# First two groups with float32r operands in both layers, and all weights turned into float16 in place during the second group

## The chip, the cores and the metric

The kernel runs on one core of one Trainium2 chip. The metric is the device time of one execution in microseconds. Engines are named as in the profile: PE multiplies matrices, PEld loads its stationary operand, DVE, ACT and POOL work on vectors, SP issues the transfers.

## The reference

`q`, `k` and `v` are float32 of shape 8 x 8 x 576 x 64 (batch, heads, positions, head size); `w_in` is 512 x 2048 and `w_out` 2048 x 512. `setup_inputs` draws `q` and `k` as normal numbers times 0.43 (0.1 x 4.30), `v` times 0.1, and the weights times one over the root of their first size.

```python
def _attn_ref(q, k, v):                      # attention inside chunks of 64 positions
    scores = scale * np.matmul(q_c, k_c.transpose(0, 1, 2, 4, 3))
    scores = scores - np.max(scores, axis=-1, keepdims=True)
    attn = np.exp(scores)
    attn = attn / (np.sum(attn, axis=-1, keepdims=True) + 1e-09)
    out = np.matmul(attn, v_c)
...
def _moe_ref(x, w_in, w_out):
    h = x @ w_in
    g = h - np.tanh(h)
    return (g @ w_out).astype(np.float32)
...
    x = np.ascontiguousarray(attn_out.transpose(0, 2, 1, 3)).reshape(B * S, H * D)
    return _moe_ref(x=x, **moe_kwargs)
```

The attention output of all heads is a token matrix `x` of 4608 x 512, and two layers with `h - tanh(h)` between them follow.

## The kernel before

The 4608 tokens are nine groups of four tiles of 128 tokens. One tile is one "pair" of chunks: its attention gives 128 rows of `x`. A group goes through 16 units `fc`, each a block of 128 hidden features. Unit `fc` of a group is 12 matmuls of the first layer (`gemm1`, L466), the step between the layers on ACT and DVE (`shrink`, L477), and 12 matmuls of the second layer (`gemm2`, L494), two units behind the first (`LAG = 2`).

Each operand of a matmul is split into a high part `h` and a low part `l`, and a product is the three matmuls h·h, h·l and l·h. There are two kinds of split. In the float16 kind, the operand is first scaled by a power of two, which takes the size of the operand (`spread` L95 or `largest` L114 along the row, then a reduction over partitions on POOL, then three small DVE instructions in `power`, L101). In the float32r kind no power is needed: `h` is a copy into float32r, `l` is the difference.

- First layer, all groups: weights `wi` and tokens `x` are float16. The weights have one power for each pair of units (`to_w`, `from_w`), the tokens of the first two groups one for each group.
- Second layer, groups 0 and 1: weights `wo` and the inner values `gh`, `gl` are float32r. From group 2 on they are float16. The conversion of `wo` runs during group 1 (`Half`, L385 on): POOL adds the two parts (`convert`, L425), ACT makes the high part, DVE the low part.

The weights come as 64-bit numbers. `weights` (L139) puts the bits together in one ACT and three DVE instructions (`merged`, L132), then splits. For the first layer this takes two units at a time, because of their common power: `spread` on ACT (L153), POOL, DVE, and then L160 and L161. For the second layer L144 and L145 make the split.

Group 0 starts while weights and tokens still arrive. The attention of the first eight pairs (groups 0 and 1) is `Early`: it works in float32 on operands laid out by the host. The last step, `result` (L268), scales by the power of the group's `v`, found by `powers` (L203) with a `spread` of each of the four `v` tiles. From pair 8 on `Late` does the attention in float16, and its steps are put between the units of the group before (`interleaved`).

The order of group 0 is the string `PLAN`. Its tokens: `a` and `v` load a pair's operands, `l` loads weights, `c` puts them together, `S`, `M` or `E`, `N` or `n`, `T` and `V` are the steps of a pair's attention, `p` the power of a group, `g` is `gemm1` with `shrink`, `h` is `gemm2`, and `F` is a number of matmuls on zeros. Up to the `|` the order of SP and PE is as written. All else is ordered by the scheduler of the language, engine by engine, and on every engine instructions then run in that order. In units 0 to 3 of group 0 the tokens come in two halves of 256 (`g0.0` and `g0.1`), later all 512 together.

When the last weights are through, the memory of the raw weights (`raw_pool`) becomes the working memory of `Late` and `Half`. `Late` then has POOL set eight tiles of zeros (L287).

Of the kernel before, what the change touches and what calls it, by code (L numbers as in the profile page):

```python
# [13 lines left out]
BF16 = mybir.dt.bfloat16  # L14
F16 = mybir.dt.float16
# [6 lines left out]
P = 128  # L22
# [15 lines left out]
RAW = 3  # L38
EARLY_FC = 8
# [11 lines left out]
a0 a1 l0.0 l1.0 v0 v1 a2 v2 v3 p0 F4 F1 l0.1 F4 S0 S1 l1.1 F1 a3 F6 l2.0 l3.0 E0 c0.0 c1.0 N0 T0 S2 F4 M1 M2 n1 c0.1 T1 N2 V0 V1 F7 S3 T2 l2.1 g0.0 c1.1 M3 V2 l3.1 N3 T3 V3 | g1.0 c2.0 c3.0 a4 l4.0 l5.0 v4 g0.1 h c2.1 Y S4 l4.1 l5.1 g1.1 a6 g2.0 E4 c3.1 h n4 a5 c4.0 c5.0 h l6.0 l7.0 c4.1 g3.0 h v6 g2.1 h l6.1 l7.1 c5.1 S5 E5 g3.1 h g4 S6 E6 h N5 c6.0 c7.0 n6 g5 l8.0 l9.0 v5 a7 v7 p1 T4 h T5 c6.1 V5 c7.1 g6 T6 V4 h S7 E7 V6 N7 l8.1 l9.1 T7 V7 Z c8.0 c9.0 l10.0 l11.0 g7 h c8.1 g8 c9.1 h g9 l10.1 l11.1 c10.0 c11.0 h c10.1 l12.0 l13.0 c11.1 l12.1 c12.0 c13.0 g10 l13.1 h c12.1 g11 l14.0 l15.0 h g12 c13.1 l14.1 l15.1 c14.0 c15.0 h g13 c14.1 c15.1 h g14 h g15 h h h  # L51
# [3 lines left out]
def attn_ffn_kernel(ctx: ExitStack, tc: tile.TileContext, qE, kE, vE, qL, kL, vL, w_in, w_out, out):  # L55

# [32 lines left out]
    to_w = const.tile([P, FC // 2], F32, name="to_w")  # L89
    from_w = const.tile([P, FC // 2], F32, name="from_w")  # L90

    def new_x():
        return tuple(xpool.tile([P, KC, MOST], F16, name=f"x{a}") for a in "hl")

    def spread(pool, a, out):  # L95

        shape = [a.shape[0], *a.shape[1:]]
        junk = pool.tile(shape, BF16, name=f"junk{math.prod(shape[1:])}", bufs=1)
        nc.scalar.activation(junk, a, AF.Abs, scale=2.0 ** -12, accum_out=out)  # L99
# [20 lines left out]
    raw_in, raw_out, w_in_f, from_x, to_x = {}, {}, {}, {}, {}  # L120

    def load_weights(pool, fc, half):
        if half:
            raw_out[fc] = pool.tile([P, DM, 2], U32, name="raw_out", bufs=RAW)
            nc.sync.dma_start(out=raw_out[fc], in_=w_out[fc])
            return
        j, i = divmod(fc, 2)
        if i == 0:
            raw_in[j] = pool.tile([P, 2, DM, 2], U32, name="raw_in", bufs=2)
        nc.sync.dma_start(out=raw_in[j][:, i], in_=w_in[fc])  # L130

    def merged(w, raw):  # L132
        low, up = raw[:, :, 0], raw[:, :, 1]
# [4 lines left out]

    def weights(pool, fc, part):  # L139
        if part:  # L140
            w = pool.tile([P, DM], U32, name="w_out", bufs=2)
            merged(w, raw_out.pop(fc))
            w = w.bitcast(F32)
            nc.scalar.copy(out=wo[fc][0], in_=w)  # L144
            nc.vector.tensor_sub(wo[fc][1], w, wo[fc][0])  # L145
            return
        j, i = divmod(fc, 2)
        if i == 0:
            w_in_f[j] = pool.tile([P, 2, DM], U32, name="w_in", bufs=2), pool.tile([P, 2], F32, name="wsum", bufs=2)
# [21 lines left out]
    class Early:  # L171
# [104 lines left out]
    class Late:  # L276
# [4 lines left out]
        def __init__(self, pool):  # L281
# [4 lines left out]
            for t in self.v16[0] + self.v16[1] + self.q16[0] + self.q16[1]:  # L286
                nc.gpsimd.memset(t, 0.0)  # L287
# [5 lines left out]
        def sums(self, g, n):  # L293
# [5 lines left out]
            if n != "v":  # L299
                spread(self.pool, some, d["sums"][:, "qkv".index(n):"qkv".index(n) + 1])  # L300
                return
# [369 lines left out]
```

## Time and profile before

| what | us |
|---|---|
| median of 3 runs | 880.99 |
| lowest, highest | 880.87, 882.39 |
| profiled execution | 883.09 |
| its span, first to last instruction | 881.3 |
| PE busy in the span | 852.8 |
| DVE busy in the span | 595.5 |
| ACT busy in the span | 490.5 |
| POOL busy in the span | 39.9 |
| mean granted TensorE clock | 0.984 |

The profiled execution lies 2.1 us above the median. Busy time counts from an instruction's start to its end; matmuls overlap in the array, so a matmul's own duration is longer than the distance between two starts, and the distance is what a stream of them costs. A clock of 1.0 stands for 2.4 GHz.

### The profile page before, as it was taken

To read this page: it belongs to the slowest core of one execution; us is meant where nothing else is said; L and a number is where in the kernel's file an instruction comes from. 1 tells how busy PE (TensorE), PEld (TensorE's weight loads), DVE (VectorE), ACT (ScalarE), POOL (GpSimd) and SP (SyncE) were. 2 spreads that over 40 slices of the span, in tenths; PEclk is the share of its full clock that TensorE was granted. 3 is DMA by queue.
4 is the path that set the end of the run, shared out by engine and by line. 5 is a ranking of instruction groups with operands and counts; after the bars stand their busy time and mean duration, and the time that the engine had idled before them with its cause. 6 is when DMAs were issued, how large, how long until landed. Compare 5 with 4: busy or idle time off the path is not lost.

```text
span 881.3 us, 13271 instructions
## 1 busy us (share of the span) xinstructions
PE 852.8 (97%) x5162; PEld 459.1 (52%) x5163; DVE 595.5 (68%) x1056; ACT 490.5 (56%) x858; POOL 39.9 (5%) x49
## 2 busy tenths in 40 slices
PE   8899897999989999999999999999999999999997
PEld 5776754566664454445444544454445444544443
DVE  5698899898796685667666866586668666543222
ACT  7589674876574664465446544654465444333222
POOL 0000003122220000000000000000000000000000
PEclk9699998999999999999999999999999999999999
DMA  9657334122132212121212121212121011001001
GB/s 233 215 158 207 120 118 146 48 72 69 40 96 65 56 50 81 52 59 49 74 59 60 49 68 64 61 49 62 71 61 26 16 45 25 13 13 48 1 1 48
DMA packets 61375, 62.73 MB, mean 71 GB/s; under 512 B 32640, under 2 KB 40832, under 8 KB 61312
## 3 DMA queue, kind: packets, MB, share of 16 engines
q1 hardware_dynamic: 61312, 61.88, 24.0%
q8 instruction: 40, 0.66, 0.3%
q14 instruction: 23, 0.19, 0.1%
HBM read 45.09 MB, written 9.44 MB: 62 GB/s over the span
## 4 chain that ended last, share of the span: by engine, by line
PE 88%; ACT 5%; DVE 3%; DMA 3%; issue 1%; SPq 1%; POOL 0%; ACTq 0%; DVEq 0%; POOLq 0%
PE ph L473 40%; PE po L499 39%; PE psa L368 2%; PE psa L334 2%; ACT junk L99 2%; PE psa L266 2%; PE psa L218 1%; DMA raw_in<-w_in 1%; DVE w_out L135 1%; DMA rawv<-vL 1%; ACT s L236 1%; DMA rawk<-kL 1%; ACT wih L160 0%; DMA vbd<-vE 0%; ACT t L481 0%
## 5 line engine op out<-in xcount | busy, mean ns | idle before, releaser
L499 PE MATMUL po<-woh,gh 128*128 128x512 f16 (+1 forms) x1024 | 321.4, 385 | 3.3 <-ACT gh L490 3.3
L499 PE MATMUL po<-woh,gl 128*128 128x512 f16 (+1 forms) x576 | 219.8, 385 | 2.4 <-DVE gl L491 2.4
L473 PEld LDWEIGHTS <-wih 128*128 128x128 f16 x1184 | 113.1, 99 | 141.7 <-ACT wih L160 10.4
L481 ACT ACTIVATE t<-ph,sig 128x512 f32<-128x512 f32 (+1 forms) x148 | 99.5, 673 | 154.1 <-PE ph L473 151.4
L482 DVE SCALAR_TENSOR_TENSOR t<-ph,sig,t 128x512 f32<-128x512 f32 (+1 forms) x148 | 108.2, 732 | 112.1 <-ACT t L481 111.9
L473 PE MATMUL ph<-xh,wih 128*128 128x512 f16 (+1 forms) x592 | 150.5, 376 | 10.2 <-ACT wih L160 8.1
L473 PE MATMUL ph<-xh,wil 128*128 128x512 f16 (+1 forms) x592 | 150.5, 377 | 0.2 <-DVE wil L161 0.2
L473 PE MATMUL ph<-xl,wih 128*128 128x512 f16 (+1 forms) x592 | 149.4, 375 | 0.0
L486 DVE SCALAR_TENSOR_TENSOR gl<-t,to_g,gh 128x512 f16<-128x512 f32 x112 | 84.0, 750 | 90.5 <-ACT gh L485 89.6
L499 PEld LDWEIGHTS <-gh 128*128 128x128 f16 x896 | 85.6, 98 | 98.7
L485 ACT ACTIVATE gh<-t,to_g 128x512 f16<-128x512 f32 x112 | 80.6, 719 | 89.4 <-PE po L499 75.2
L473 PEld LDWEIGHTS <-wil 128*128 128x128 f16 x592 | 58.1, 99 | 67.7 <-issue 2.1
L499 PEld LDWEIGHTS <-gl 128*128 128x128 f16 x448 | 43.8, 98 | 52.9
L499 PE MATMUL po<-wol,gh 128*128 128x512 f32 x128 | 51.1, 399 | 0.0
L316 ACT ACTIVATE q16h<-rawq,to 64x512 f16<-64x512 f32 x56 | 40.2, 719 | 11.9 <-DVE to L112 9.8
L317 DVE SCALAR_TENSOR_TENSOR q16l<-rawq,to,q16h 64x512 f16<-64x512 f32 x56 | 43.7, 780 | 1.4
L326 DVE SCALAR_TENSOR_TENSOR v16l<-rawv,to,v16h 64x512 f16<-64x512 f32 x56 | 41.9, 749 | 1.1 <-ACT xh L371 0.2
L325 ACT ACTIVATE v16h<-rawv,to 64x512 f16<-64x512 f32 x56 | 40.0, 714 | 1.5 <-PE psa L368 0.8
L354 ACT CAST a<-s 128x512 f16<-128x512 f32 x28 | 17.3, 617 | 34.2 <-DVE s L348 34.0
L342 ACT ACTIVATE s<-s,exp 128x512 f32<-128x512 f32 x28 | 19.9, 712 | 20.8 <-DVE s L341 20.8
L499 PEld LDWEIGHTS po<-woh,gh 128*128 128x128 f32 x128 | 24.5, 191 | 11.5 <-ACT gh L490 5.5
L499 PEld LDWEIGHTS po<-woh,gl 128*128 128x128 f32 x128 | 24.3, 190 | 8.6 <-DVE gl L491 3.1
(122 smaller groups left out, 938.8 us busy)
## 6 DMA issues: line engine op xcount, KB each, us to landing
out<-t SPq DMA_DIRECT2D x36, 256.0 KB, 2.1
raw_in<-w_in SPq DMA_DIRECT2D x16, 512.0 KB, 5.0
raw_out<-w_out SPq DMA_DIRECT2D x16, 512.0 KB, 4.2
rawq<-qL SPq DMA_DIRECT2D x28, 256.0 KB, 2.7
rawk<-kL SPq DMA_DIRECT2D x28, 256.0 KB, 3.0
rawv<-vL SPq DMA_DIRECT2D x28, 256.0 KB, 2.6
qbd<-qE SPq DMA_DIRECT2D x16, 128.0 KB, 4.4
k<-kE SPq DMA_DIRECT2D x8, 256.0 KB, 4.4
```

The source lines that it names most:

```text
L99: nc.scalar.activation(junk, a, AF.Abs, scale=2.0 ** -12, accum_out=out)
L316: nc.scalar.activation(qh[r, :, r], q[r], AF.Copy, scale=to[r, 0:1])
L317: nc.vector.scalar_tensor_tensor(out=ql[r, :, r], in0=q[r], scalar=to[r, 0:1], in1=qh[r, :, r], op0=ALU.mult, op1=ALU.subtract)
L325: nc.scalar.activation(vh[r, :, r], v[r], AF.Copy, scale=to[r, 2:3])
L326: nc.vector.scalar_tensor_tensor(out=vl[r, :, r], in0=v[r], scalar=to[r, 2:3], in1=vh[r, :, r], op0=ALU.mult, op1=ALU.subtract)
L342: nc.scalar.activation(s, s, AF.Exp, scale=d["exp"])
L473: nc.tensor.matmul(ph, lhsT=wi[fc // 2][a][:, fc % 2, kc * P:(kc + 1) * P], rhs=x[b][:, kc, cols], start=(k == 0), stop=(k == 3 * KC - 1))
L481: nc.scalar.activation(t, ph, AF.Tanh, scale=sig)
L482: nc.vector.scalar_tensor_tensor(out=t, in0=ph, scalar=sig, in1=t, op0=ALU.mult, op1=ALU.subtract)
L485: nc.scalar.activation(gh, t, AF.Copy, scale=self.to_g)
L486: nc.vector.scalar_tensor_tensor(out=gl, in0=t, scalar=self.to_g, in1=gh, op0=ALU.mult, op1=ALU.subtract)
L499: nc.tensor.matmul(self.po[t], lhsT=gg[a][:, ts], rhs=self.wo[fc][b], start=(fc == 0 and i == 0), stop=(fc == FC - 1 and i == 2))
```

## The change

Groups 0 and 1 now use float32r in both layers, so nothing in them needs a power. The powers of the early tokens (`p`) and of the pairs of units are gone, and with them the `spread` calls on `v` and on the first layer's weights, the reductions on POOL, and the scaling in `shrink`. Both weight blocks of a unit are one tile of 1024 columns, put together and split in the same instructions (`weights`; some units in two parts of 512, as `PLAN` says). ACT forms the sums of squares of all 32 weight blocks (L588 of the new file) for one power for all of `w_in` and one for all of `w_out`.

In group 1 `convert` now turns both blocks of a unit into float16, each into the memory of its own high part, with the memory of a low part as room for the sum. It starts earlier (after `gemm2` of the same unit) and has 32 additions on POOL instead of 16, 32 high parts on ACT and 32 low parts on DVE. Two low parts that come free (units 0 and 1) become the second set of zeroed tiles for `Late`, which starts with one set. `Late` also shares more memory: the raw `q` lies in the low part of group 0's tokens, `k16` has one buffer instead of two, and the transposed weights of the attention take a buffer of `s`. From group 2 on the matmuls have the forms that they had.

```diff
 PLAN = """
-a0 a1 l0.0 l1.0 v0 v1 a2 v2 v3 p0 F4 F1 l0.1 F4 S0 S1 l1.1 F1 a3 F6 l2.0 l3.0 E0 c0.0 c1.0 N0 T0 S2 F4 M1 M2 n1 ...
+a0 a1 l0.0 l0.1 a2 v2 F4 F1 v0 F4 S0 v1 l1.0 S1 l1.1 F1 c0 F1 a3 F6 l2.0 c1 F1 E0 N0 T0 S2 F4 l3.0 M1 M2 n1 ...
...
+                wt[fc][i] = pool.tile([P, 2, DM], F32R, name=f"w{a}{fc}")
...
     def new_x():
-        return tuple(xpool.tile([P, KC, MOST], F16, name=f"x{a}") for a in "hl")
+        return tuple(xpool.tile([P, KC, MOST], F32R, name=f"x{a}") for a in "hl")
...
+        h, l = (t[:, parts] for t in wt[fc])
+        nc.scalar.copy(out=h, in_=w.bitcast(F32))
+        nc.vector.tensor_sub(l, w.bitcast(F32), h)
...
-            nc.scalar.activation(xh[:, :, ts], ps, AF.Copy, scale=to)
-            nc.vector.scalar_tensor_tensor(out=xl[:, :, ts], in0=ps, scalar=to, in1=xh[:, :, ts], op0=ALU.mult, op1=ALU.subtract)
+            nc.scalar.copy(out=xh[:, :, ts], in_=ps)
+            nc.vector.tensor_sub(xl[:, :, ts], ps, xh[:, :, ts])
...
-            for t in self.v16[0] + self.v16[1] + self.q16[0] + self.q16[1]:
+            for t in v + q:
                 nc.gpsimd.memset(t, 0.0)
...
         def convert(self, fc):
-            w = self.pool.tile([P, DM], F32, name="whole", bufs=2)
-            nc.gpsimd.tensor_add(w, wo[fc][0].bitcast(F32), wo[fc][1].bitcast(F32))
-            half = wo_pool[fc].tile([P, DM], F32R, name=f"woh{fc}").bitcast(F16).rearrange("p (a n) -> p a n", a=2)
...
+            for part in range(2):
+                nc.gpsimd.tensor_add(w[part], h[:, part].bitcast(F32), l[:, part].bitcast(F32))
+            half = half_w[fc] = w_pool[fc].tile([P, 2, DM], F32R, name=f"wh{fc}").bitcast(F16).rearrange("p part (a n) -> p part a n", a=2)
+            for part in range(2):
+                to = self.to[:, part:part + 1]
+                nc.scalar.activation(half[:, part, 0], w[part], AF.Copy, scale=to)
+                nc.vector.scalar_tensor_tensor(out=half[:, part, 1], in0=w[part], scalar=to, in1=half[:, part, 0], op0=ALU.mult, op1=ALU.subtract)
...
+            if self.half:
+                nc.scalar.activation(t, ph, AF.Tanh, scale=self.sig)
+                nc.vector.scalar_tensor_tensor(out=t, in0=ph, scalar=self.sig, in1=t, op0=ALU.mult, op1=ALU.subtract)
+            else:
+                nc.scalar.activation(t, ph, AF.Tanh)
+                nc.vector.tensor_sub(t, ph, t)
...
+    for fc in range(FC):
+        for part in range(2):
+            nc.scalar.activation(junk, wt[fc][0][:, part].bitcast(F32), AF.Square, accum_out=sums_w[part][:, fc:fc + 1])
...
         if g == 1:
-            for k, fs in half.steps().items():
-                at[k] += fs
+            half.powers()
+            for fc in range(FC):
+                at[2 * fc + 2 * LAG + 1].append(lambda fc=fc: half.convert(fc))
+            at[2 * LAG + 4].append(lambda: att.room(half.spare(0), half.spare(1)))
```

Three places of the new order, engine by engine. The first is ACT at the start of group 0, from the copy of pair 0's transposed weights (`aT`) to the first `xh`. Before, these rows were:

```order
L258 COPY aT<-psa 128x512
L99 ACTIVATE junk_176,vsum_175<-vbd_129 128x1024
L99 ACTIVATE junk_256,wsum<-w_in 128x512
L99 ACTIVATE junk_178,vsum_175<-vbd_130 128x1024
L99 ACTIVATE junk_262,wsum<-w_in 128x512
L249 ACTIVATE s<-s,sm 128x64 x4
L160 ACTIVATE wih_70<-w_in,to_w 128x512 x2
L99 ACTIVATE junk_180,vsum_175<-vbd_131 128x1024
L249 ACTIVATE s<-s,sm 128x64 x2
L99 ACTIVATE junk_182,vsum_175<-vbd_132 128x1024
```

In the new kernel, ACT has these rows at the same place (L215 is the old L249, L224 the old L258, L137 the split of the weights, L239 the new `xh`):

```order
L132 ACTIVATE w<-raw 128x1024
L224 COPY aT<-psa 128x512
L215 ACTIVATE s<-s,sm 128x64 x8
L137 CAST wh_70<-w 128x1024
L224 COPY aT<-psa 128x512
L198 ACTIVATE s<-s 128x512
L588 ACTIVATE junk,sums_86<-wh_70 128x512
L239 CAST xh<-psa 128x4x128
```

The eight products L215 now stand together right behind the first `aT`; no sum of `v` or of weights stands ahead of them or between them.

The second place is POOL in group 1. Before, behind the eight memsets came single additions:

```order
L425 TENSOR_TENSOR whole<-woh_71,wol_73 128x512
L425 TENSOR_TENSOR whole<-woh_74,wol_75 128x512
L106 ISA
L106 ISA xtop<-sums 128x3
L106 ISA htop<-both 128x2
L425 ISA
L425 TENSOR_TENSOR whole<-woh_77,wol_79 128x512
```

Now these stand there, behind the first four memsets and the reductions for the weights' powers:

```order
L405 TENSOR_TENSOR s<-wh_70,wl_71 128x512 x2
L106 ISA
L106 ISA xtop<-sums 128x3
L405 ISA
L405 TENSOR_TENSOR s<-wh_72,wl_73 128x512 x2
L259 MEMSET wl_1655 128x1024 x2
L259 MEMSET wl_1656 128x1024 x2
L405 TENSOR_TENSOR s<-wh_74,wl_75 128x512 x2
L405 TENSOR_TENSOR wl_1742<-wh_76,wl_77 128x512 x2
```

The additions come in twos, one for each weight block, and four of the eight memsets have moved in between them.

The third place is DVE in group 1, around the first steps of pair 8's softmax. Before (L430 is the low part of `convert`, L482 and L491 belong to `shrink`):

```order
L430 SCALAR_TENSOR_TENSOR woh_2204<-whole,to_half,woh_2204 128x512
L430 SCALAR_TENSOR_TENSOR woh_2246<-whole,to_half,woh_2246 128x512
L436 RECIPROCAL undo_g<-to_g 128x1
L437 TENSOR_TENSOR undo_g<-undo_g,from_half 128x1
L491 TENSOR_TENSOR gl<-t,gh 128x512
L430 SCALAR_TENSOR_TENSOR woh_2282<-whole,to_half,woh_2282 128x512
L482 SCALAR_TENSOR_TENSOR t<-ph,sig,t 128x512
L491 TENSOR_TENSOR gl<-t,gh 128x512
L340 TENSOR_REDUCE mx<-psa 128x8
```

And now (L410 is the low part of `convert`, L461 and L470 belong to `shrink`, L290 and L299 to `split`):

```order
L410 SCALAR_TENSOR_TENSOR wh_1619<-s,to_w,wh_1619 128x512 x2
L299 SCALAR_TENSOR_TENSOR wl_1655<-rawv,to,wl_1655 64x8x64 x2
L470 TENSOR_TENSOR gl<-t,gh 128x512
L313 TENSOR_REDUCE mx<-psa 128x8
L290 SCALAR_TENSOR_TENSOR wl_1656<-xl,to,wl_1656 64x8x64 x2
L410 SCALAR_TENSOR_TENSOR wh_1680<-s,to_w,wh_1680 128x512 x2
L410 SCALAR_TENSOR_TENSOR wh_1745<-wl_1742,to_w,wh_1745 128x512 x2
L461 TENSOR_TENSOR t<-ph,t 128x512
```

Between two instructions of `shrink` (L470 and L461) there are now seven others, four of them of `convert`.

## Rows read from the trace of the kernel before

**Rows 1.** Busy time of each engine in four stretches: group 0 up to its longest stop, the end of group 0, group 1, groups 2 to 8. Columns: stretch in us, its length, busy us and instructions of PE, PEld, DVE, ACT and POOL, granted clock, DMA share, GB/s.

```profile
39.30:143.90 104.60, 98.30 (x565) 71.36 (x562) 94.35 (x208) 82.14 (x217) 6.25 (x11) 1.00 0.52 164
143.90:163.30 19.40, 14.11 (x55) 7.75 (x55) 18.46 (x29) 12.48 (x31) 7.40 (x8) 0.82 0.00 1
163.30:262.60 99.30, 94.71 (x574) 60.27 (x574) 86.66 (x147) 69.47 (x111) 21.98 (x17) 0.97 0.24 68
262.60:881.30 618.70, 613.95 (x3841) 296.37 (x3839) 374.64 (x624) 302.07 (x441) 1.86 (x5) 1.00 0.17 48
```

**Rows 2.** The chain that ended last, in order of time (start, us, what): pieces of group 1, the start of group 2 and of group 8.

```profile
174.33 2.77 PE po L499 x12
177.11 2.61 PE ph L473 x12
...
262.64 7.92 PE ph L473 x36
270.56 2.59 PE po L499 x12
...
793.67 7.77 PE ph L473 x36
```

**Rows 3.** The timeline of all engines at the start (start, us, engine, line, what, idle time before and its releaser): ACT behind the first transposes, PE up to the first unit.

```profile
17.02 1.06 ACT L99 ACTIVATE junk<-vbd 128x1024 bf16<-128x1024 f32 x1
...
21.70 1.33 ACT L160 ACTIVATE wih<-w_in,to_w 128x512 f16<-128x512 f32 x2 [0.31 <-DVE to_w L112]
...
26.64 0.48 PE L168 MATMUL psa<-ident,s 128*128 128x128 f32 x1 [1.56 <-ACT s L249]
...
26.91 6.93 PE L266 MATMUL psa<-aT,vbd 128*128 128x64 f32 x32
...
33.62 3.19 PE L571 MATMUL ph<-warm 128*128 128x512 bf16 x7
...
36.61 2.40 PE L218 MATMUL psa<-k,qbd 128*128 128x64 f32 x16
...
39.29 0.60 PE L473 MATMUL ph<-xh,wih 128*128 128x256 f16 x4
```

**Rows 4.** Who PE waited for up to 176 us: us in total, times, the longest.

```profile
PE ph L473 <- ACT wih L160: 8.1, 4, 5.3
PE psa L168 <- ACT s L249: 5.5, 3, 2.8
```

**Rows 5.** The timeline of PE at the end of group 0, around its longest stop.

```profile
149.40 2.31 PE L473 MATMUL ph<-xh,wih 128*128 128x512 f16 x5 [5.29 <-ACT wih L160]
151.51 1.91 PE L473 MATMUL ph<-xh,wil 128*128 128x512 f16 x4
153.22 1.20 PE L473 MATMUL ph<-xl,wih 128*128 128x512 f16 x4
```

**Rows 6.** The timeline of DVE at the same time.

```profile
141.68 5.52 DVE L135 TENSOR_SCALAR w_out<-w_out 128x512 uint32<-128x512 uint32 x1
```

**Rows 7.** The timeline of POOL at the same time: the first and the sixth of the memsets that ran without a gap.

```profile
141.44 1.02 POOL L287 MEMSET v16h<- 128x1024 f16 x1
...
145.90 1.02 POOL L287 MEMSET q16l<- 128x1024 f16 x1
```

**Rows 8.** The timeline of PE from the last second-layer matmuls of group 0 into group 1.

```profile
163.26 1.04 PE L473 MATMUL ph<-xh,wil 128*128 128x512 f16 x4
...
169.90 1.18 PE L473 MATMUL ph<-xh,wih 128*128 128x512 f16 x4 [2.15 <-DVE t L482]
...
173.93 0.63 PE L499 MATMUL po<-woh,gh 128*128 128x512 f32 x1
```

**Rows 9.** The timeline of PE in group 0: float32 matmuls of the attention, and behind them a first-layer half unit in float16.

```profile
63.68 2.46 PE L218 MATMUL psa<-k,qbd 128*128 128x64 f32 x20
65.97 0.60 PE L473 MATMUL ph<-xh,wih 128*128 128x256 f16 x4
66.41 0.60 PE L473 MATMUL ph<-xh,wil 128*128 128x256 f16 x4
```

**Rows 10.** Groups of weight loads over the whole span: line, engine, operation, names, shape, count, busy us, mean ns of one, idle us before.

```profile
L473 PEld LDWEIGHTS <-wih 128*128 128x128 f16 x1184 | 113.1, 99 | 141.7 <-ACT wih L160 10.4 <-issue 9.9 <-ACT woh L144 0.3
...
L499 PEld LDWEIGHTS po<-woh,gh 128*128 128x128 f32 x128 | 24.5, 191 | 11.5 <-ACT gh L490 5.5 <-issue 0.3
```

**Rows 11.** Groups of DVE instructions up to 176 us, in the same columns.

```profile
L116 DVE TENSOR_REDUCE largest_in<-wih 128x1 f32<-128x1024 f16 x8 | 9.5, 1210 | 0.0
```

**Rows 12.** Groups of DVE instructions in group 1 (163.3 to 262.6 us).

```profile
L430 DVE SCALAR_TENSOR_TENSOR woh<-whole,to_half,woh 128x512 f16<-128x512 f32 x15 | 11.9, 797 | 0.2 <-ACT woh L429 0.2
...
L317 DVE SCALAR_TENSOR_TENSOR q16l<-rawq,to,q16h 64x512 f16<-64x512 f32 x12 | 10.9, 912 | 0.3
...
L348 DVE TENSOR_TENSOR s<-s,sm 128x512 f32<-128x512 f32 x4 | 3.7, 925 | 0.1
...
L355 DVE TENSOR_TENSOR a<-s,a 128x512 f16<-128x512 f32 x4 | 2.8, 688 | 0.1
```

**Rows 13.** The POOL additions in group 1, as a group.

```profile
L425 POOL TENSOR_TENSOR whole<-woh,wol 128x512 f32<-128x512 f32 x14 | 20.8, 1493 | 59.8 <-DVE woh L430 25.6 <-ACT gh L490 14.6 <-DVE v16l L326 7.1
```

**Rows 14.** The timeline of all engines late in group 1: a DVE group and the POOL additions beside it.

```profile
254.32 3.52 DVE L317 SCALAR_TENSOR_TENSOR q16l<-rawq,to,q16h 64x512 f16<-64x512 f32 x2
254.35 2.95 POOL L425 TENSOR_TENSOR whole<-woh,wol 128x512 f32<-128x512 f32 x2 [7.13 <-DVE v16l L326]
```

More of the change, by code (lines that the diff above doesn't have):

```diff
@@ L14 @@
 BF16 = mybir.dt.bfloat16
+U8 = mybir.dt.uint8
 F16 = mybir.dt.float16
@@ L38 @@
 RAW = 3
+WS = 2
 EARLY_FC = 8
@@ L117, in largest, with load_weights, weights @@
         nc.vector.tensor_scalar_mul(out, out, 2.0 ** -12)
[L120 to L133, printed above, removed]
+    raws, ws, from_x, to_x = {}, {}, {}, {}
+    def load_weights(pool, fc, part):
+        if part == 0:
+            raws[fc] = pool.tile([P, 2, DM, 2], U32, name="raw", bufs=RAW)
+        nc.sync.dma_start(out=raws[fc][:, part], in_=(w_in, w_out)[part][fc])
+    def weights(pool, fc, parts):
+        if fc not in ws:
+            ws[fc] = pool.tile([P, 2, DM], U32, name="w", bufs=WS)
+        r, w = raws[fc][:, parts], ws[fc][:, parts]
+        low, up = r[:, :, :, 0], r[:, :, :, 1]
         nc.scalar.activation(w.bitcast(F32), up.bitcast(F32), AF.Abs, scale=2.0 ** -112)
@@ new lines, in powers @@
+            for part in range(2):
+                nc.vector.reduce_max(out=both[:, part:part + 1], in_=sums_w[part], axis=AX.X)
+            nc.vector.tensor_scalar_mul(both, both, 2.0 ** -12)
+            power(self.pool, "w", both, self.to, self.back)
+            whole = self.pool.tile([P, FC], F32, name="whole")
+            nc.gpsimd.partition_all_reduce(whole, sums_w[0], channels=P, reduce_op=bass_isa.ReduceOp.add)
+            nc.vector.reduce_max(out=self.to_h, in_=whole, axis=AX.X)
+            nc.vector.tensor_scalar_mul(self.to_h, self.to_h, math.sqrt(KC))
@@ L472, in gemm1 @@
                 for kc in range(KC):
[L473 removed]
+                    nc.tensor.matmul(ph, lhsT=self.weight(fc, 0, a)[:, kc * P:(kc + 1) * P], rhs=x[b][:, kc, cols], start=(k == 0), stop=(k == 3 * KC - 1))
                     k += 1
@@ L498, in gemm2 @@
                 for i, (a, b) in enumerate(((0, 0), (0, 1), (1, 0))):
-                    nc.tensor.matmul(self.po[t], lhsT=gg[a][:, ts], rhs=self.wo[fc][b], start=(fc == 0 and i == 0), stop=(fc == FC - 1 and i == 2))
+                    nc.tensor.matmul(self.po[t], lhsT=gg[a][:, ts], rhs=self.weight(fc, 1, b), start=(fc == 0 and i == 0), stop=(fc == FC - 1 and i == 2))
         def run(self, units, at, ahead=None):
@@ L586, in step @@
         elif kind == "c":
-            for k in (0, 1) if part is None else (part,):
-                weights(raw, n, k)
+            weights(raw, n, slice(0, 2) if part is None else slice(part, part + 1))
         elif kind == "g":
@@ L612, in attn_ffn_kernel @@
         step(token)
+    junk = raw.tile([P, DM], U8, name="junk", bufs=1)
+    for fc in range(FC):
+        for part in range(2):
+            nc.scalar.activation(junk, wt[fc][0][:, part].bitcast(F32), AF.Square, accum_out=sums_w[part][:, fc:fc + 1])
     ff.finish()
```

156 lines of the change are left out of this document (51 added, 105 removed).

## The prediction

> **What bounds the kernel now.** I first split the span at group borders. From 262.6 us on PE is busy 613.95 of 618.7 us [rows 1], and group 2 starts at 262.64, group 8 at 793.67 [rows 2]: 531.03 us for six groups, 88.5 each. There nothing but PE counts. The change leaves the forms of these matmuls alone, and DVE (374.64) and ACT (302.07) have room. So the time moves only by what happens before 262.64 us, and the question is when group 2 can start.
>
> That stretch has three parts. At the start PE waits for operands until its first unit at 39.29 us [rows 3]. In group 0 up to 143.9 us PE is busy 98.30 of 104.6 us and DVE 94.35 [rows 1]: PE is the bound, DVE close behind. From 143.9 to 163.3 PE is busy 14.11 of 19.4 us, with one stop of 5.29 us [rows 1, 5]. Group 1 takes 99.3 us, PE 94.71, DVE 86.66 busy [rows 1]. So I sum PE's path, and look in each part whether another engine becomes the bound.
>
> **Price of float32r in the first layer.** In group 1, 12 first-layer matmuls in float16 take 2.61 us and 12 second-layer ones in float32r 2.77 us [rows 2]: 0.16 us more for a unit, 13 ns for a matmul. Both have 512 moving columns, so a full unit of the first layer should now cost 2.77 as well. Group 0 has 12 full units: +1.9 us. Group 1 has 16: +2.6 us. Units 0 to 3 of group 0 come in halves of 256 columns, 8 halves of 12 matmuls = 96. In float16 four of them take 0.44 us, 110 ns each [rows 9]. No row shows float32r with 256 columns. The low bound is the attention in float32, which also loads its stationary operand at full width: 20 in 2.29 us, 114 ns [rows 9]; the high bound is the duration of a float32r weight load, 191 ns against 99 ns in float16 [rows 10], if a load could not overlap the one before. The attention's rows speak for overlap, and I add the 13 ns of the full unit to the 110: about 122 ns, +1.2 us (bounds +0.4 and +7.8). Nothing hides these terms, PE being the bound.
>
> **The start.** Before the first unit PE waited 5.5 us, in three pieces, with the transposes of L168 for ACT's product L249 [rows 4], the last time at 26.64 [rows 3]. Between the pieces ACT ran sums over `v` of 1.06 us and the scaled split L160, 1.33 us for two [rows 3]. The new order has none of that ahead of the eight products, and from there to the first unit it keeps the same attention steps. From 26.91 to 39.29 PE did 12.4 us of work in a fixed order [rows 3], which moves forward as a whole. The gain lies between 0 and 5.5 us; I take 5.0, because the second pair's operands and weights come through the same transfers as before, and PE has two more matmuls on zeros.
>
> **Waits in group 0.** PE waited 8.1 us for the scaled split L160 [rows 4], 5.29 of it in one stop [rows 5]. That split needed the power, hence POOL and DVE. DVE stood in one shift for 5.52 us from 141.68 [rows 6], while POOL ran six memsets without a gap from 141.44 to 146.9 [rows 7]. After the stop the clock was low: nine matmuls from 149.40 to 153.22 took 3.82 us [rows 5] where 9 x 0.2175 = 1.96 is usual, 1.9 us lost (the stretch's granted clock is 0.82 [rows 1]). So the stop cost 7.2 us. In the new kernel no unit waits for POOL, and POOL sets four tiles, not eight, ahead of group 1. They become free with the raw weights of unit 14, while DVE still has unit 15 to put together: its shift can again meet them, for at most 4 x 0.9 = 3.6 us. I take 1.0, as DVE has the shift queued and need not lose the race: -6.2. Of the other 2.8 us of waits for L160 I count half as gone, since weights still have to be put together: -1.4. The sums of squares on ACT take the place of as many sums over the weights and come cheaper than those plus the sums over `v`.
>
> Group 0 in sum: -5.0 - 6.2 - 1.4 + 1.9 + 1.2 = -9.5 us.
>
> **Group 1.** PE's own work: 94.71 busy, less 1.4 for the low clock after its stop at 169.90 (12 matmuls took 4.03 us to 173.93 [rows 8], 2.61 usual), plus 2.6 = 95.9 us. DVE: 86.66 busy [rows 1]; `convert` now makes 32 low parts, of which the order puts the last two in group 2, instead of 15 here: 15 more x 0.80 [rows 12] = +12.0. Two maxima over the weights, 1.21 each [rows 11], and their small instructions go: -3.4. That is 95.3 us: as much as PE. On top come meetings with POOL. Its additions grow from 14 to 30 in this stretch [rows 13]. What one costs DVE: the twelve L317 had 912 ns in the mean [rows 12], and without the two of 3.52 us [rows 14] 742; four products L348 took 925 ns where four L355 of the same size took 688 [rows 12]; fifteen L430 had 797 [rows 12], 55 above those 742. Together 2.0 + 0.9 + 0.8 = 3.7; with the small instructions, which I estimate at a third of that, 4.9 us for 14 additions, 0.35 each. Sixteen more: +5.6. So DVE needs 101 us, PE can't go faster than that, and with 2 us for the instructions that bunch (seven others between two of `shrink`) group 1 lasts 103: +3.7 us. ACT gets 15 more high parts of about 0.67 (two of L160 took 1.33 [rows 3]), 10 us on 69.47 busy [rows 1], so it has cover.
>
> **Sum.** -9.5 + 3.7 = -5.8 us. The profiled execution goes from 883.09 (span 881.3) to 877.3, the median, 2.1 us below it, from 881.0 to 875.2.
>
> **Rivals.**
>
> *DVE and POOL shut each other out in group 1 (slower).* In rows 14 two DVE instructions beside two additions took 3.52 us instead of 1.48: 1.0 us for each addition. If that is the price whenever one meets another, DVE needs 95.3 + 16 + 2 = 113.3 us, group 1 grows by 14.0, and the time is 881.0 - 9.5 + 14.0 = 885.5. The point from which this rival decides is 0.75 us for an addition: there group 1 takes 109 us and eats the whole gain. For it: additions now come in pairs, and many of the added DVE instructions read two tiles of SBUF. Against it: most of the 14 additions cost far less, 0.35 in the mean; but DVE then had 12.6 us of idle time in which to be missed. Chance 0.17. The Trainium skill speaks for this rival: its page "SBUF — State Buffer", section "Who interferes with whom", says that a DVE instruction with two inputs in SBUF and a GpSimd instruction that reads SBUF exclude each other for the whole instruction. Rows 14 agree with it.
>
> *The additions fall into gaps.* Then PE bounds group 1: 95.9 + 2 = 98 us, -1.3, and the time is 881.0 - 10.8 = 870.2; with a few more of group 0's small waits gone, 867. For it: converted weights are needed only in group 2, and PE runs two units behind, so DVE may be late by some us without PE stopping. Against it: DVE's order is fixed, and `convert` stands between the instructions of `shrink`. Chance 0.20.
>
> *Half units go at the speed of their weight loads.* At 191 ns instead of 122 the 96 matmuls cost 6.6 us more: 881.8. Against it stand the 114 ns of the attention. Chance 0.10.
>
> *The powers were not what held group 0.* If the first unit waits for the weights instead (both blocks of a unit must now be there and put together), the 5.0 us at the start do not come: 880.2. Against it: the weight loads stand in SP's queue where they stood, and the first weights' split began at 21.70, before the tokens' products from 26.91 [rows 3]. Chance 0.08.
>
> **How the numbers follow.** The forecast, 875.2, has 0.45 (872 to 879). About 0.2% (1.8 us) is what a measurement here can tell from no change, so faster means below 879.2. The forecast and the gap case make 0.65, and some of the last two rivals and of a mild form of the first end there too: 0.69 faster. Same 0.13, slower 0.18. The range reaches from 865, the gap case with a better start, to 886, just above the first rival.
>
> **What would show it.** In the new profile the first unit should start near 34 us; 12 first-layer matmuls of groups 0 and 1 take 2.77 us, four half ones about 0.49; no stop of 5 us stands near the end of group 0, which ends near 154; DVE is busy over 95% of group 1, with durations of its two-input instructions stretched beside additions; group 2 starts near 257, and groups 2 to 8 take 88.5 each. I am wrong if group 1 takes over 107 us or under 99, if half units take more than 150 ns a matmul, or if groups 2 to 8 change.

## The result and the profile after

The changed kernel takes **887.9 us** in the median of 5 runs (885.75 to 889.29), the kernel before 882.39 in the 5 runs taken with them (880.87 to 883.04): ratio **1.0064, 95% interval 1.004 to 1.0087**, so slower by 0.6%, where the prediction takes 0.2% as the least that a measurement here can tell. The forecast was 875.2. The profiled execution took 889.29 us, its span is 887.3.

Group 1 of the kernel before starts at 163.26 - 4 x 0.2175 = 162.39 [rows 8] and group 2 at 262.64 [rows 2]; the other borders are in the rows below. So the spans part like this:

| us | before | after | forecast | measured |
|---|---|---|---|---|
| up to the first unit | 39.3 | 26.4 | -5.0 | -12.9 |
| group 0 | 123.1 | 115.0 | -4.5 | -8.1 |
| group 1 | 100.2 | 115.2 | +3.7 | +15.0 |
| groups 2 to 8 | 618.7 | 630.7 | 0 | +12.0 |
| span | 881.3 | 887.3 | -5.8 | +6.0 |

The gains, 21.0 us up to the end of group 0, were more than twice the forecast. They were lost again, with 6 us more, in two places: in group 1, and in groups that the change was not thought to touch.

Busy time of the engines after, in group 0, group 1 and groups 2 to 8 (columns as in [rows 1]):

```profile
26.40:141.40 115.00, 111.85 (x616) 94.67 (x615) 97.06 (x166) 90.10 (x238) 4.46 (x6) 1.00 0.55 168
141.40:256.60 115.20, 100.94 (x577) 79.15 (x575) 100.39 (x140) 66.13 (x104) 50.93 (x36) 0.96 0.20 52
256.60:887.30 630.70, 616.95 (x3841) 295.87 (x3840) 380.99 (x642) 307.90 (x452) 4.34 (x7) 1.00 0.17 49
```

In group 0 PE has 3 us of gaps in 115. In group 1 it has 14. In groups 2 to 8 PE's busy time grew by 3 us and the stretch by 12.

The timeline of PE after: the start, then units and stops in group 1, and group 2's first units.

```profile
18.65 3.88 PE L232 MATMUL psa<-aT,vbd 128*128 128x64 f32 x32
22.58 1.46 PE L544 MATMUL ph<-warm 128*128 128x512 bf16 x6
...
26.41 0.72 PE L449 MATMUL ph<-xh,wh 128*128 128x256 f32 x4
26.97 0.64 PE L449 MATMUL ph<-xh,wl 128*128 128x256 f32 x4
27.45 0.64 PE L449 MATMUL ph<-xl,wh 128*128 128x256 f32 x4
...
184.54 1.19 PE L449 MATMUL ph<-xh,wh 128*128 128x512 f32 x4 [3.09 <-DVE t L461]
...
235.17 1.07 PE L449 MATMUL ph<-xh,wl 128*128 128x512 f32 x4
236.07 1.07 PE L449 MATMUL ph<-xl,wh 128*128 128x512 f32 x4
...
244.04 0.80 PE L478 MATMUL po<-wh,gh 128*128 128x512 f32 x1 [4.17 <-ACT gh L469]
...
252.35 0.50 PE L478 MATMUL po<-wh,gh 128*128 128x512 f32 x1 [3.07 <-ACT gh L469]
...
256.64 5.79 PE L449 MATMUL ph<-xh,wh 128*128 128x512 f16 x24
```

Against [rows 3] the 32 products started 8.3 us earlier and took 3.88 us, not 6.93, and the matmuls on zeros behind them 1.46, not 3.19: 8.3 + 3.05 + 1.7 is the 12.9 at the start, within 0.2. Four half matmuls are 0.48 us apart (120 ns each) and four full ones 0.90 (225 ns): both prices of float32r came close to the forecast (0.49 us and 2.77 for twelve).

Who PE waited for in group 1 after (us in total, times, the longest), and the groups of DVE instructions there (columns as in [rows 12]):

```profile
PE po L478 <- ACT gh L469: 7.2, 2, 4.2
PE ph L449 <- DVE t L461: 5.9, 2, 3.1
```

```profile
L410 DVE SCALAR_TENSOR_TENSOR wh<-wl,to_w,wh 128x512 f16<-128x512 f32 x24 | 23.5, 1008 | 0.1
L470 DVE TENSOR_TENSOR gl<-t,gh 128x512 fp32r<-128x512 f32 x16 | 14.0, 878 | 5.2 <-ACT gh L469 5.1
L461 DVE TENSOR_TENSOR t<-ph,t 128x512 f32<-128x512 f32 x16 | 10.7, 674 | 5.7 <-ACT t L460 5.7
```

L461, which reads PSUM and one tile of SBUF, takes its usual time (687 ns in run 4 below, which has no additions); L410 and L470, which read two tiles of SBUF, are stretched (742 and 687 there). The timeline of POOL and DVE before the first stop, of DVE and ACT before the one at 244.04, and of ACT before the one at 252.35, shows it one by one:

```profile
173.23 13.04 POOL L405 TENSOR_TENSOR wl<-wh,wl 128x512 f32<-128x512 f32 x8
177.14 3.38 DVE L410 SCALAR_TENSOR_TENSOR wh<-s,to_w,wh 128x512 f16<-128x512 f32 x2
180.44 3.44 DVE L410 SCALAR_TENSOR_TENSOR wh<-wl,to_w,wh 128x512 f16<-128x512 f32 x2
183.80 0.68 DVE L461 TENSOR_TENSOR t<-ph,t 128x512 f32<-128x512 f32 x1
...
239.78 2.48 POOL L405 TENSOR_TENSOR wl<-wh,wl 128x512 f32<-128x512 f32 x2 [2.45 <-PE po L478]
239.93 1.14 DVE L320 TENSOR_SCALAR sm<-sm 128x8 f32<-128x8 f32 x1
241.11 1.70 DVE L321 TENSOR_TENSOR s<-s,sm 128x512 f32<-128x512 f32 x1
242.85 0.62 ACT L327 CAST a<-s 128x512 f16<-128x512 f32 x1 [5.82 <-DVE s L321]
243.37 0.61 ACT L469 CAST gh<-t 128x512 fp32r<-128x512 f32 x1
...
247.41 1.91 ACT L99 ACTIVATE a<-xl 128x2048 uint8<-128x2048 f32 x1 [2.19 <-DMA s<-a]
```

Beside eight additions in a row, four L410 took 1.7 us each, and the L461 behind them, which PE waits for, came at 183.80. At 241 the stretched product L321 is late, ACT stands for it 5.82 us in its fixed order, and `gh`, which PE waits for, is queued behind. The stop at 252.35 has another head: ACT stood 2.19 us for a transfer that reads `a`, then ran the sums over q and k (L99), and `gh` came behind them. So a part of group 1's loss hangs on that transfer as well; how much, no run tells apart.

That the new splits had to wait for POOL's sums explains little of it: DVE stood 0.1 us ahead of its L410, and ACT 2.9 us in all ahead of its high parts (L409).

The timeline of all engines at the border of groups 2 and 3 after (the last line is the third unit of group 3):

```profile
332.22 1.91 ACT L99 ACTIVATE a<-xl 128x2048 uint8<-128x2048 f32 x1 [1.57 <-DMA s<-a]
334.25 1.91 ACT L99 ACTIVATE a<-rawk 128x2048 uint8<-128x2048 f32 x1
...
344.47 0.60 PE L478 MATMUL po<-wh,gh 128*128 128x512 f16 x2 [0.72 <-ACT gh L464]
345.65 0.39 PE L478 MATMUL po<-wh,gl 128*128 128x512 f16 x1 [0.58 <-DVE gl L465]
347.66 0.33 SPq L263 DMA_DIRECT2D rawv<-vL  x1
348.11 4.46 SPq L510 DMA_DIRECT2D out<-t  x4
351.45 0.75 DVE L502 TENSOR_SCALAR t<-po,undo_g 128x512 f32<-128x512 f32 x1 [2.71 <-DMA out<-t]
352.45 0.69 ACT L457 ACTIVATE t<-ph,sig 128x512 f32<-128x512 f32 x1 [4.39 <-DMA out<-t]
353.98 2.75 PE L449 MATMUL ph<-xh,wh 128*128 128x512 f16 x12 [0.81 <-DVE t L458]
```

Read it from the top. The sums over the next group's raw q and k (L99) throw their product into tile `a`, the one buffer that the transposing transfer of the last pair reads, so ACT stands 1.57 us for that transfer. All splits of the next group's first pairs come behind the sums and fill ACT and DVE until the group ends. `gh` is late by 0.72 us and `gl` by 0.58. The second pair's `rawv` can be loaded only at 347.66; on SP's queue the output waits behind it, holds the buffers of `t`, and so the first tanh of the new group, for which PE waits 0.81. Third units are then 90.6 us apart, not 88.5.

### The profile page after: what moved, and what is told of

Same layout as the page of the kernel before. It is cut to its first block, busy times and chain, and to the rows that moved or that the text cites. A ratio compares the mean times of both kernels' runs of the same rounds, so it can differ in the third digit from the quotient of the medians.

```text
span 887.3 us, 13178 instructions
## 1 busy us (share of the span) xinstructions
PE 853.9 (96%) x5163; PEld 487.2 (55%) x5165; DVE 597.3 (67%) x980; ACT 482.5 (54%) x840; POOL 60.4 (7%) x55
## 4 chain that ended last, share of the span: by engine, by line
PE 68%; DVE 17%; DMA 5%; ACT 4%; issue 4%; SPq 1%; POOL 0%; ACTq 0%; POOLq 0%; DVEq 0%
PE ph L449 32%; PE po L478 30%; DVE wh L410 2%; DMA s<-a 2%; DMA out<-t 2%; PE psa L307 2%; PE psa L341 1%; PE psa L232 1%; ACT a L99 1%; DVE q16l L290 1%; DVE gl L470 1%; DVE v16l L299 1%; PE psa L184 1%; DVE t L461 1%; DMA k<-kE 1%
## 5 line engine op out<-in xcount | busy, mean ns | idle before, releaser
L449 PE MATMUL ph<-xh,wh 128*128 128x512 f16 (+2 forms) x1488 | 344.1, 379 | 9.3 <-DVE t L461 5.9
L478 PE MATMUL po<-wh,gh 128*128 128x512 f16 (+1 forms) x1024 | 319.2, 383 | 12.6 <-ACT gh L469 8.8
L478 PE MATMUL po<-wh,gl 128*128 128x512 f16 (+1 forms) x576 | 221.2, 385 | 2.9 <-DVE gl L465 2.9
L449 PEld LDWEIGHTS <-wh 128*128 128x128 f16 x1344 | 130.3, 98 | 157.9 <-issue 4.7
L457 ACT ACTIVATE t<-ph,sig 128x512 f32<-128x512 f32 x112 | 76.5, 683 | 139.1 <-PE ph L449 119.9
L458 DVE SCALAR_TENSOR_TENSOR t<-ph,sig,t 128x512 f32<-128x512 f32 x112 | 83.4, 745 | 96.6 <-ACT t L457 96.3
L464 ACT ACTIVATE gh<-t,to_g 128x512 f16<-128x512 f32 x112 | 80.7, 721 | 98.2 <-PE po L478 85.4
L478 PE MATMUL po<-wl,gh 128*128 128x512 f32 x128 | 51.4, 402 | 0.0
L405 POOL TENSOR_TENSOR wl<-wh,wl 128x512 f32<-128x512 f32 x26 | 40.3, 1568 | 38.1 <-PE po L478 31.0
L449 PE MATMUL ph<-xh,wl 128*128 128x512 f32 (+1 forms) x144 | 36.3, 374 | 0.1
L449 PE MATMUL ph<-xl,wh 128*128 128x512 f32 (+1 forms) x144 | 36.2, 374 | 0.0
L449 PEld LDWEIGHTS ph<-xh,wh 128*128 128x128 f32 x144 | 24.8, 188 | 13.2 <-DVE t L461 7.2
L470 DVE TENSOR_TENSOR gl<-t,gh 128x512 fp32r<-128x512 f32 (+1 forms) x36 | 25.7, 713 | 7.1 <-ACT gh L469 6.8
```

The lines of the kernel that those rows point to most:

```text
L405: nc.gpsimd.tensor_add(w[part], h[:, part].bitcast(F32), l[:, part].bitcast(F32))
L449: nc.tensor.matmul(ph, lhsT=self.weight(fc, 0, a)[:, kc * P:(kc + 1) * P], rhs=x[b][:, kc, cols], start=(k == 0), stop=(k == 3 * KC - 1))
L457: nc.scalar.activation(t, ph, AF.Tanh, scale=self.sig)
L458: nc.vector.scalar_tensor_tensor(out=t, in0=ph, scalar=self.sig, in1=t, op0=ALU.mult, op1=ALU.subtract)
L464: nc.scalar.activation(gh, t, AF.Copy, scale=self.to_g)
L470: nc.vector.tensor_sub(gl, t, gh)
```

## Experiments

Each ratio is to runs of the kernel before that were taken beside the run. An edit also lets the scheduler order the engines' work anew, so each run shows its edit together with the order that came with it.

**1 and 2. A junk tile of its own, then more tiles of their own.** After group 1 the low parts of the weights are free, and one of them takes the junk:

```diff
-                junk = self.pool.tile([P, 2, H * CH], F16, name="a", bufs=1).bitcast(U8)...
+                junk = self.own["junk"] if "junk" in self.own else (as before)
...
+        if g == 2:
+            att.own["junk"] = half.spare(2)[0].bitcast(U8).rearrange("p (b n) -> p b n", b=MOST // P)
```

> One edit to the changed kernel: from group 2 on the product that the sums over raw q and k throw away goes to a spare weight tile, no longer to the tile `a` that the transposing transfer reads. Theory A (the shared tile holds the sums of the next group behind the last pair's transfer, so that the splits bunch at the group's end): groups 2 to 6 last 88.5 us again in place of 90.7, 5 x 2.2 = 11 us less, and the end of group 1, where ACT stood 2.2 us for that transfer and the sums then held the next tanh, gets 3 to 5 us shorter: 872 to 874. Rival B (the one buffer of k16, or aT in the buffers of s, makes the border longer): groups 2 to 6 stay at 90.7, 885 to 888.

> As the run with a junk tile of its own, and from group 2 on k16 has a second buffer and aT a tile of its own, both spare weight tiles. Theory A: these two add nothing, 872 to 874, within 0.2% of the run with the junk tile alone. Rival B: only this run brings groups 2 to 6 back to 88.5 us each, some 874, while the junk tile alone stays at 885 to 888.

Measured: 882.99 us, ratio 1.0015 [0.9999, 1.0031], and 882.34, 1.0008 [0.9997, 1.0019]. Both times lie between the theories, and the profile says why. The chain of `own_junk` and POOL's timeline in its group 1:

```profile
141.73 8.43 PE ph L449 x36
260.63 7.79 PE ph L449 x36
349.13 7.77 PE ph L449 x36
437.61 7.77 PE ph L449 x36
```

```profile
233.72 0.39 POOL L106 PARTITION_ALL_REDUCE xtop<-sums  x1 [12.61 <-PE po L478]
241.17 13.16 POOL L405 TENSOR_TENSOR wl<-wh,wl 128x512 f32<-128x512 f32 x8 [7.07 <-issue]
```

Groups 2 to 6 last 88.5 us again: theory A holds for them, and k16 and aT do nothing (B falls). Its other half, a shorter group 1, fails: group 1 now lasts 118.9 us instead of 115.2. Freed from the transfer, the sums for group 3 moved forward inside group 1, on ACT from 247.41 to 215.55 us. POOL's all-reduce stands in its queue ahead of eight additions. It starts when the last of its sums is there (the row names PE, but L117 on DVE ends only at 233.51), the first addition follows 7.07 us behind it, and all eight run in one stretch of 13.2 us.

**3. The junk in `a`, in the kernel before.**

```diff
-                spread(self.pool, some, d["sums"][...])
+                junk = self.pool.tile([P, 2, H * CH], F16, name="a", bufs=1) (as bytes)
+                nc.scalar.activation(junk, some, AF.Abs, scale=2.0 ** -12, accum_out=d["sums"][...])
```

> The kernel before with this one part of the change: the sums over raw q and k throw their product into tile `a`, as bytes, in place of a tile of their own. Theory A: groups 2 to 6 take 90.7 us instead of 88.5, and the end of group 1 gets some us longer: 882 + 11 + 0 to 4 = 893 to 897. Rival B: the time stays at 882, since k16 and aT keep their own buffers here.

Measured: 889.87 us, ratio 1.0084 [1.0059, 1.0108]. PE at two borders, and ACT ahead of the first:

```profile
331.17 1.91 ACT L301 ACTIVATE a<-rawq 128x2048 uint8<-128x2048 f32 x1 [1.21 <-DMA aT<-a]
...
353.39 1.02 PE L474 MATMUL ph<-xh,wih 128*128 128x512 f16 x4 [1.27 <-DVE t L483]
...
444.66 1.02 PE L474 MATMUL ph<-xh,wih 128*128 128x512 f16 x4 [1.29 <-DVE t L483]
```

This one edit makes the border stops in the other kernel too: third units 91.3 us apart. The time is below the forecast of 893 to 897, as my guess for group 1 was wrong in sign. The sums, held back from 214.26 us to 248.34, take splits behind them out of group 1 (DVE runs 131 instructions there, 147 before), and the third unit of group 2 starts at 261.98, where 262.64 + 2 x 2.59 = 267.8 was the place before. So the shared tile moves work from group 1 to the later borders.

**4. No additions; 6. half of them; 7. both losses undone.**

```diff
-            for part in range(2):
-                nc.gpsimd.tensor_add(w[part], h[:, part].bitcast(F32), l[:, part].bitcast(F32))
+            w = [l[:, part].bitcast(F32) for part in range(2)]
```

> The changed kernel without POOL's 32 additions: ACT and DVE make the float16 weights from the low part alone, so the sum of high and low part is left out and the converted weights are not the right ones; every other instruction stays. Theory C (DVE and POOL shut each other out: in group 1 of the changed kernel 30 splits L410 took 1.02 us in the mean where undisturbed ones take 0.74, and with L470, L299, L290, L293, L321 and L320 some 22 us of DVE's time are stretched): group 1 gets 10 to 15 us shorter, as PE's own 96 us and the sums' wait at its end then bound it: 873 to 878. Rival D (the bunched instructions of the splits and the wait of the sums for the transfer at the end of group 1 make it long, not the additions): less than 4 us are gained, 884 to 888.

> The changed kernel with 16 of POOL's 32 additions: those for w_out are left out, and its float16 weights are made from the low part alone, so they are not the right ones; every other instruction stays. A price for each addition (18.4 us for 32 in the run without any, 0.57 each): 887.9 - 9 = 879. A threshold (DVE's 80.7 us without additions and 0.7 for each of 16 make 92, less than PE's 97.6, so DVE is no bound any more): group 1 lasts some 99 us and the time is 871 to 873.

> Both edits: a junk tile of its own from group 2 on, and none of POOL's 32 additions (the float16 weights are made from the low part alone and are not the right ones). If the two losses are separate causes, group 1 lasts 97.6 us as without additions, groups 2 to 6 last 88.5, and the time is 869.5 - 11 = 858.5. If the junk tile's loss in group 1 does not come by way of the additions, group 1 stays some 4 us longer: 862 to 863.

Measured: 869.48 us, 0.9856 [0.9838, 0.9874]; 872.5, 0.991 [0.9879, 0.9941]; 858.3, 0.9751 [0.971, 0.9791]. Group 1 without additions and with half of them (columns as in [rows 1]), and DVE's costliest group without. The 97.6 us and 80.7 us of the expectations come from a stretch up to 239.0 us, but group 2 starts at 236.36:

```profile
141.20:236.40 95.20, 95.20 (x577) 76.56 (x576) 78.11 (x142) 66.50 (x104) 4.86 (x6) 1.00 0.23 63
```

```profile
142.70:242.10 99.40, 97.17 (x578) 77.93 (x577) 82.97 (x147) 64.97 (x103) 23.32 (x20) 0.98 0.22 65
```

```profile
L404 DVE SCALAR_TENSOR_TENSOR wh<-wl,to_w,wh 128x512 f16<-128x512 f32 x30 | 21.3, 742 | 0.1
```

Theory C holds, and more is gained than it forecast: group 1 lasts 95.2 us, 20.0 less, not 10 to 15. D falls. Without additions PE has no gap and the same splits take 742 ns. The price is not a fixed one for each addition: sixteen cost 3 to 5 us, thirty-two 18. DVE's own busy time says the same. With the fourteen additions that lie in the stretch it is 83.0 us, 4.9 more than with none, 0.35 for each; with thirty it is 100.4, some 22 more, 0.7 for each. So the price itself rises with the number. The threshold's time came out, though it had reckoned with 92 us of DVE. With half of them the additions stand one by one, 2 to 8 us apart, and the splits (L411 there) take 743 ns in the mean; in the changed kernel they come in twos and once in a row of eight. That the bunching makes the price is read from the rows; no run varies it alone. With both losses undone, 858.3 came where 858.5 was expected: the two are separate causes and together cost 28 to 30 us.

**5. The junk tile one group later.** As `own_junk`, with `if g == 3`.

> As the run with a junk tile of its own, but only from group 3 on: the sums for group 3, which the first run drew into group 1, go on sharing `a`. Theory F (the junk tile's gain of 11 us in groups 2 to 6 was given back in group 1, where the early sums put POOL's all-reduce ahead of eight additions, which then ran as one stretch of 13.2 us beside DVE's splits): group 1 lasts 115 us as in the changed kernel, groups 2 to 6 last 88.5, and the time is 887.9 - 11 = 877. Rival G (the lead of group 0 is lost somewhere later whatever the sums do): 882 to 884 again.

Measured: 876.46 us, ratio 0.9957 [0.9938, 0.9977].

```profile
254.57 7.94 PE L449 MATMUL ph<-xh,wh 128*128 128x512 f16 x36
```

Group 2 starts at 254.57, so group 1 lasts 113.0 us, and later borders are 88.5 apart. Theory F holds; this keeps the changed kernel's arithmetic and is already faster than the kernel before, by 0.4%.

**8 and 11. The powers of the start, in the kernel before.** The sums over `v` (and in 11 those over `w_in`), their all-reduces and what follows become a memset of 1.0.

> The kernel before with this one part of the change: the power for the tokens of groups 0 and 1 is the constant 1, so the sums over v on ACT, the two all-reduces behind them and what DVE makes of them are left out; the float16 operands stay. Theory H (these sums stood between the pieces of the normalising that PE's transposes waited for, and the waits left PE at the low clock, where the 32 products that follow took 6.9 us against 3.9 in the changed kernel): the first unit starts 7 to 10 us earlier, near 30, and the time is 882 - 7 = 873 to 877. Rival I (the weights' power and split hold the first unit as well): it starts at 35 or later, and the time is 878 to 882.

> The kernel before with both powers of the start replaced by the constant 1: the sums over v, as in the run without them, and also the sums over w_in and the all-reduce behind them, so that no scaled split of group 0 waits for POOL; the operands stay float16. If these powers are what held the first unit (35.7 us without the sums over v, 26.4 in the changed kernel), it starts at 27 to 31, the stop of 5.3 us for L160 near the end of group 0 is gone, and the time is 873.2 - 4 to 6 - 7 = 860 to 864. If the rest of the 9 us lies in the new order of the start, the first unit stays at 34 to 36, and only the stop goes: 866 to 868.

Measured: 873.18 us, 0.9911 [0.9876, 0.9946], and 859.64, 0.9767 [0.9709, 0.9826]. PE at the start and at the stop near the end of group 0 without the sums over `v`, then at the start and at the first unit of group 1 without either power:

```profile
23.42 6.71 PE L265 MATMUL psa<-aT,vbd 128*128 128x64 f32 x32
...
35.66 0.60 PE L472 MATMUL ph<-xh,wih 128*128 128x256 f16 x4
...
142.25 2.31 PE L472 MATMUL ph<-xh,wih 128*128 128x512 f16 x5 [5.31 <-ACT wih L160]
```

```profile
20.71 6.93 PE L265 MATMUL psa<-aT,vbd 128*128 128x64 f32 x32
...
32.50 0.60 PE L472 MATMUL ph<-xh,wih 128*128 128x256 f16 x4
...
143.00 1.04 PE L472 MATMUL ph<-xh,wih 128*128 128x512 f16 x4
```

The first unit moved by 3.6 us, not 7 to 10, and with the weights' power by 6.8: each of H and I names a half. The products still ran at the low clock (granted 0.59 from 23 to 27 us and 0.50 from 27 to 33 in the first of the two, 0.50 from 18 to 27 in the second), so it was not the sums alone that lowered it. The other 6.1 us of the 12.9 remain for the new order of the start: 2.1 by an earlier begin of the products (18.65 against 20.71), most of the rest by products (3.88 us, not 6.93) and zeros at full clock. That the stop for L160 went in 11 and stayed, 5.3 us long, in 8 bears out that the split waited for the weights' power. The times fell by more than the first unit moved. In run 11 group 0 lasts 143.00 - 32.50 = 110.5 us, 12.6 less than before, and group 1, up to 238.94, 4.3 less. So the powers cost more behind the first unit than ahead of it.

**9, 10 and 12. A version without additions that leaves nothing out.** If the high part of a weight fits float16, the float16 pair is a scaled copy of either part, and nothing need be added:

```diff
-        nc.scalar.copy(out=h, in_=w.bitcast(F32))
+        half = raws[fc].rearrange("p a n two -> p a (n two)").bitcast(F16)[:, parts, :DM]
+        nc.scalar.copy(out=half, in_=w.bitcast(F32))
+        (nc.vector.tensor_copy if fc % 2 else nc.scalar.copy)(out=h, in_=half)
...
+                nc.scalar.activation(made[part][:, 0], h[:, part].bitcast(F32), AF.Copy, scale=to)
+                nc.vector.tensor_scalar_mul(made[part][:, 1], l[:, part].bitcast(F32), to)
```

`made` is the low-part tile that the block before left free; the junk tile is as in `own_junk`. Unit 0 has no block before it; its float16 weights are made in `s` and copied back by DVE. `Late` gets its second set of zeroed tiles two steps later. The line with `fc % 2` is that of run 10.

> A version without additions that computes the reference in full. In group 0 ACT makes the high part of a weight in two copies, by way of float16, so that a float16 number with the power of two holds it whole and the low part is what is left; in group 1 the float16 weights are then a scaled copy of the high part (ACT) and one of the low part (DVE), each into the tile that the weights before left free, and POOL adds nothing. The sums throw their product into a spare weight tile from group 2 on. Theory C and A together: group 1 lasts 97 to 99 us and groups 2 to 6 last 88.5, as in the run with neither loss (858.3), and group 0 grows by 0 to 3 us, since ACT gets 16 copies of 1.03 more on 89.8 of 115 us: 858 to 862. Rival J: the second copy delays each block of weights and keeps the raw tiles longer, so PE waits for weights in group 0, which grows by over 5 us: 864 to 870.

> As the version without additions, but DVE makes every second one of the second copies in group 0. If ACT is what group 0 waits for (rival J), this is faster than the run with all copies on ACT by some us; if DVE is the closer of the two (97 of 115 us busy, ACT 90), it is slower by 1 to 3 us; if neither, the two are within 0.2%, 858 to 862.

> As the version without additions, with all 16 second copies of group 0 on DVE. Group 1 began at 152.6 us with all of them on ACT and at 147.9 with half, against 141.4 in the changed kernel. If ACT was what group 0 waited for, it begins near 143 to 145 now and the time is 858 to 860. If DVE, 100 of 115 us busy with half of them, is the bound by now, group 0 gets longer again and the time is 864 to 868. If both are near their limit, the time is within 0.3% of the half version, 860 to 865.

Measured: 868.75 us, 0.9858 [0.9822, 0.9894]; **862.66, 0.9787 [0.9751, 0.9823]**; 864.24, 0.9806 [0.9788, 0.9824]. Group 0 and group 1 of the second:

```profile
26.40:147.90 121.50, 114.01 (x613) 95.69 (x613) 103.35 (x178) 97.77 (x249) 3.69 (x4) 0.99 0.49 154
147.90:243.00 95.10, 95.10 (x577) 76.84 (x577) 79.96 (x161) 73.08 (x115) 5.34 (x8) 1.00 0.28 79
```

Group 1 has no gap on PE in 95.1 us. Rival J was right of the first: group 1 started at 152.6 us with all copies on ACT, at 147.9 with half on each, and no earlier with all on DVE (group 2 at 243.53, against 243.00). With all of them on DVE, ACT is free of them, but PE then waits in group 0 for DVE's splits (3.6 us) and for `gh` from ACT (2.9 us). Moving copies only changes what PE waits for, and in run 10 group 0 stays 6.5 us longer than in the changed kernel. Even so run 10 beats both kernels, by 2.1 and, dividing the two ratios, some 2.8%.

## Why the prediction was wrong

Three steps were off, and two of them nearly cancel: up to the end of group 0 the change gave 11.5 us more than forecast, and group 1 took 11.3 more. What is left of the miss is the 12.0 us of groups 2 to 8.

*The start and group 0* went the right way and too short. "I take 5.0" was mis-sized: 12.9, of which 3.6 for the sums over `v` and 3.2 for the weights' power are shown by runs 8 and 11; the higher clock and the new order are the rest, read from rows alone. The "12.4 us of work in a fixed order", which was to move forward as a whole, took 7.8. What holds the clock low in one order of the start and not in the other stays open. The rest of group 0 gave 8.1 us, not 4.5: no stop of over 1.1 us is left, so the half that was to stay of the other waits, and the 1.0 us for a second meeting with the memsets, were too cautious. Run 11 puts the powers at 12.6 us there, where the sum had 7.6. Both float32r prices held.

*Group 1* is the first step that failed. PE's own work held, 95.9 us in the sum and 95.2 in run 4. DVE's busy time came out as forecast, 100.4 us against 101, but by luck, as two of its parts were wrong and cancel. The sum held 95.3 - 14 x 0.35 = 90.4 us without any meeting, and run 4 has 78.1, mostly because 20 splits for the next group stand in the stretch, 29 before. An addition was put at 0.35 us, which is what it costs with fourteen in the stretch (run 6); with thirty it cost 0.7. The step that broke is "with 2 us for the instructions that bunch": DVE stood idle for 14.8 us. The rows read as if an engine that needs 100 us of another's 95.2 can't be filled when its work comes in bursts and its order is fixed; that is argued, while the runs show that the loss goes with the additions. The first rival names the right mechanism, but its 113.3 us lie near the 115.2 by luck too: it had DVE busy for all of them, at 1.0 us for an addition. The Trainium skill's rule cited there ("SBUF — State Buffer", section "Who interferes with whom") is borne out by L410 at 1008 ns beside additions and 742 without, and by L461 untouched at 674.

*Groups 2 to 8* are the second. "The change leaves the forms of these matmuls alone, and DVE and ACT have room. So the time moves only by what happens before 262.64 us" looked at shares of busy time and at forms, not at which tile an instruction writes. The new kernel's `sums` writes the junk to `a` (the diff shown ahead leaves that line out), and a transfer reads `a`. That costs 12 us, as the runs 1 and 3 show from both sides. No rival had it; only the last of the signs ("or if groups 2 to 8 change") allowed for it.

With 858.3 us without either loss, in a run that leaves the weights' sums out, and 862.66 in run 10, which leaves nothing out, the idea for groups 0 and 1 was worth more than forecast; the time went into a tile and a queue.

## What to carry to other kernels

A scratch output that nobody reads is still a write: where it shares a buffer with a transfer's source, its instruction and all that is queued behind it wait for that transfer. Look up who last reads each tile that a change merges, above all where engines have room.

When one engine's work would come to a hundred per cent of another's, count it as late, and look for the bursts; here half of the additions gave back nearly all. Undo one loss at a time with the order of the instructions beside it, since a wait that goes can move its work to a worse place.

## What the runs showed of the hardware

A small DVE instruction was caught by an addition as well: L320 on 128x8 numbers, with one input, took 1.14 us at 239.93, and 0.15 us at 190.00, where no addition ran. Its mean in group 1 was 718 ns, and 165 in the run without additions.

Behind an all-reduce POOL stood 6.8 to 7.4 us before its next addition, at all three places of the changed kernel where one followed, and 7.07 in run 1. Why is not shown.

PE's low clock (0.50, the 1.2 GHz level) lay in other stretches of the start with each order: from 27 to 33 us in the kernel before, from 10.5 to 14 in the changed one, from 18 to 27 in run 11. In the kernel before, PE was busy for 0.84 of the four us ahead of that (mean clock 0.61 there); in the changed one it was busy all through the 2.5 us ahead (mean 0.57).
